# A 1536-row down projection moved from the start of a fused attention and GLU kernel into its dense end

## The chip, the cores and the metric

The kernel runs on one core of one Trainium2 chip. The metric is device time in microseconds (us) from launch to end; a run's time is compared with runs of the kernel before on the same chip. TensorE (PE) multiplies, with its weight loads (PEld) beside it; VectorE (DVE), ScalarE (ACT) and GpSimd (POOL) work elementwise; SyncE (SP) and GpSimd issue transfers (DMA), each from a queue of its own, in order.

## What is computed

```python
def _A_ref(x, k_cache, v_cache, wq, wo):
    B, Sq, D = x.shape                      # 1, 2048, 640
    Hq, Dh = 32, 192
    Hkv, Sk = k_cache.shape[1], k_cache.shape[2]
    W = min(4096, max(256, Sk // 4))        # 512
    ...
    scores = jnp.einsum("bhqd,bhkd->bhqk", q, k) * (Dh ** -0.5)
    p = _softmax(scores, axis=-1)
    o = jnp.einsum("bhqk,bhkd->bhqd", p, v)
    return (lambda x, *d: x.transpose(*d))(o, 0, 2, 1, 3).reshape(B, Sq, Hq * Dh) @ wo

def _B_ref(x, w_gate, w_up, w_down):        # D 640, F 1536
    g = jnp.einsum("bsd,df->bsf", x, w_gate)
    u = jnp.einsum("bsd,df->bsf", x, w_up)
    h = _sigmoid(g) * u
    return jnp.einsum("bsf,fd->bsd", h, w_down)

x = A_x
xn = _layernorm(x, axis=-1)
s = _A_ref(xn, A_k_cache, A_v_cache, A_wq, A_wo)
g = _silu(_B_ref(xn, B_w_gate, B_w_up, B_w_down))
return x + s * g
```

## The kernel before

The order of the work is written out by hand; every engine runs its instructions in program order.

The opening makes the gate g. It goes through four blocks of 512 rows (`s` = 0 to 3, loop over `NST`). In a block, twelve chunks of 128 hidden columns (`f`) are worked one after the other: ten matmuls into a pair of PSUM banks (line 469), a sigmoid on ScalarE (474), and on VectorE a product with the up half (475) into `hT_sb`, two buffers of which exist. Four bank pairs are used in turn, so TensorE's chunk f+4 waits for the VectorE product of chunk f. Then four row tiles of 128 rows go through the down projection (517): 24 matmuls each with `hT_sb` as the stationary operand, of 512 and 128 columns; sigmoid and product make the gate (524, 525), and GpSimd's queue writes it to `gB_d` in DRAM (541).

Other work is laid into these loops. The layer norm of the next block's four row tiles: statistics (`ln_stats`) at f = 5 to 8, the square root on ScalarE (`ln_rstd`, 352, with a table load before and after it) at f = 9, and at f = 10 and 11 the apply (359) and the transposes by DMA (428) into `xnT[s]`. Blocks 1 and 3 share one buffer `x_odd`; the apply has three output buffers, so the fourth apply waits for the first transpose. The largest absolute value of W_q is found in sixteen pieces of 1920 columns a partition (`scan_load`, `scan_fold`), all by VectorE; `set_scale` sends the per-partition result through DRAM to all partitions, and `set_scale2` makes of it a power of two, `w_up`, by which W_q goes to fp16. In block 3, W_q's first group is scaled and split: for each of its chunks ScalarE scales (240) and copies, VectorE makes sums (`sum_w`), and one more ScalarE copy (245) waits for such a sum. `swap` and `sum_x` prepare sums of x for a seven-product form of the query projection.

Attention runs in sixteen stages `r` (eight groups of heads g by two halves of the rows pi): query products (571), scores (665), exponent (669), values (679). Its output goes through transposes on SyncE's queue into `oT_d` in DRAM (`store_o`). ScalarE also sums the absolute values of W_o and v (724, 728), from which the scales of the dense end come.

The dense end multiplies the attention output by W_o. It takes sixteen steps m: eight pairs of row tiles for each half of the 6144 inner columns. A pair is a 2 by 2 block product made with seven products instead of eight (Winograd's form of Strassen's method), in fp16: four quads A11 to A22 (each 128 by 12 by 128) are loaded two steps ahead (`load_quads`), scaled by ScalarE (782), and summed by VectorE (`sum_quad`: S1 to S4); seven `product`s of twelve 320-column matmuls (950) fill three banks; `keep` (957) takes partial results out by ScalarE, `result` (969, 977, 979) adds them by VectorE. W_o's blocks are loaded, scaled and summed likewise (`load_op`, `scale_op`, `sum_op`). The first eight steps leave sums in `acc`; `prep` multiplies them by the gate read back from `gB_d` and adds x; the last eight finish the rows.

## Time and profile before

| | us |
|---|---|
| three runs: median (lowest to highest) | 878.44 (878.37 to 878.54) |
| the profiled execution, its own time | 878.02 |
| its span, first to last instruction | 876.2 |
| TensorE's mean granted clock | 1.000 |
| opening, up to the last down projection's end | 0 to 164.4 |
| attention | 164.4 to 689.4 |
| dense end | 689.4 to 876 |

In a list of groups a line reads: source line, engine, operation, output<-input, shapes, count, then busy time in us and mean ns of one. In a timeline it reads: start us, duration us, engine, line, operation, and in brackets the idle time of the engine just before and what ended it. Instructions of one engine overlap by about a tenth of a us, so the start of the next one tells what an instruction costs. A q after an engine's name is its transfer queue. The opening, by windows of ten us:

```profile
core 0: us, PE busy (x) PEld busy (x) DVE busy (x) ACT busy (x) POOL busy (x), PEclk, DMA share, GB/s
20.00:30.00 10.00, 10.00 (x48) 4.54 (x47) 7.03 (x17) 3.16 (x6) 0.00 (x0) 1.00 1.09 346
...
60.00:70.00 10.00, 10.00 (x48) 4.55 (x47) 9.75 (x15) 3.74 (x6) 0.09 (x1) 1.00 0.80 254
...
140.00:150.00 10.00, 10.00 (x48) 4.56 (x47) 8.21 (x14) 7.36 (x11) 1.19 (x2) 1.00 0.53 116
```

Columns are each engine's busy us and instructions, TensorE's granted clock, the mean busy share of the transfer engines and what they moved.

### The profile page before, as it was taken

Reading aid. Unit: us, or ns where it says so; the run is one execution under the profiler, and the core shown is the slowest. Engines: PE = TensorE matmul, PEld = TensorE weight load, DVE = VectorE, ACT = ScalarE, POOL = GpSimd, SP = SyncE. Lnnn points to the kernel's source line nnn. Section 1 sums busy time; section 2 is a strip of 40 time slices with the busy share of each in tenths; the row PEclk is TensorE's granted clock in tenths of the full one; section 3 lists DMA queues with packets and bytes.
Section 4 is the critical chain, followed back from the end, with each engine's and each line's share of the span. In section 5 each row is a group of like instructions: output and inputs, shape, how many; then the busy total and the mean of one; then the engine's idle time right before and its main releaser. Section 6 shows DMA issues by size and latency. Waiting matters only on the chain.

```text
span 876.2 us, 18804 instructions
## 1 busy us (share of the span) xinstructions
PE 870.4 (99%) x7605; PEld 564.1 (64%) x7605; DVE 670.4 (77%) x1088; ACT 576.7 (66%) x693; POOL 231.0 (26%) x326
## 2 busy tenths in 40 slices
PE   9999999999999999999999999999999999999998
PEld 5545454567757757757757757757757777777775
DVE  4879947677767767767767767777978868888986
ACT  4323347775887887797797797777485566666662
POOL 0050212582334334334334334334000000000000
PEclk9999999999999999999999999999999999999999
DMA  9994465229698898798898798689998998557641
GB/s 279 269 271 114 107 118 124 93 56 169 152 217 139 196 221 149 182 226 158 185 214 170 172 215 148 150 196 206 219 271 126 231 367 263 181 173 266 198 136 36
DMA packets 246935, 161.34 MB, mean 184 GB/s; under 512 B 158848, under 2 KB 231808, under 8 KB 246848
## 3 DMA queue, kind: packets, MB, share of 16 engines
q1 hardware_dynamic: 238304, 132.90, 62.3%
q0 software_dynamic: 8544, 27.24, 14.2%
q8 instruction: 59, 0.97, 0.5%
q14 instruction: 28, 0.23, 0.1%
HBM read 93.65 MB, written 30.41 MB: 142 GB/s over the span
## 4 chain that ended last, share of the span: by engine, by line
PE 98%; DVE 1%; DMA 0%; ACT 0%; issue 0%; DVEq 0%
PE ps_all L571 21%; PE ps_all L950 20%; PE ps_all L679 20%; PE ps_all L665 19%; PE ps_all L469 11%; PE ps_all L517 6%; PE ps_all L382 1%; DVE stats L344 0%; DVE arm L933 0%; DMA x_sb<-in_A_x_dram 0%; DVE arm L979 0%; DVE arm L977 0%; DVE xn L359 0%; ACT mid L397 0%; PE ps_all L395 0%
## 5 line engine op out<-in xcount | busy, mean ns | idle before, releaser
L669 ACT ACTIVATE E<-ps_all 128x1024 bf16<-128x1024 f32 x256 | 251.1, 1021 | 120.7 <-PE ps_all L665 120.0
L665 PE MATMUL ps_all<-qT,kT 64*128 64x512 bf16 x1536 | 198.2, 377 | 0.0
L679 PEld LDWEIGHTS <-E 128*128 128x128 bf16 x2048 | 169.7, 98 | 8.1 <-issue 8.1
L679 PE MATMUL ps_all<-v_sb,E 128*128 128x193 bf16 x2048 | 174.0, 247 | 0.0
L609 DVE TENSOR_TENSOR qT<-ps_all,qp 128x512 bf16<-128x512 f32 x174 | 115.5, 687 | 47.8 <-PE ps_all L571 36.5
L592 DVE COPY qp<-ps_all 128x512 f32<-128x512 f32 x150 | 100.6, 687 | 47.7 <-PE ps_all L571 47.6
L665 PEld LDWEIGHTS <-kT 64*128 64x128 bf16 x1536 | 84.9, 94 | 79.4 <-issue 4.4
L686 DVE TENSOR_TENSOR o_st<-ps_all,rden 128x768 bf16<-128x768 f32 x128 | 122.5, 957 | 4.4
L950 PEld LDWEIGHTS <-mid 128*128 128x128 f16 x996 | 97.3, 98 | 37.9
L571 PE MATMUL ps_all<-mid 64*128 64x512 f16 (+1 forms) x840 | 106.0, 376 | 0.0
L571 PE MATMUL ps_all<-mid,arm 64*128 64x512 f16 (+1 forms) x840 | 105.6, 376 | 0.0
L571 PEld LDWEIGHTS <-mid 64*128 64x128 f16 x840 | 48.8, 94 | 43.5 <-issue 1.2
L571 PEld LDWEIGHTS <-arm 64*128 64x128 f16 x840 | 47.0, 94 | 44.7 <-issue 0.3
L782 ACT ACTIVATE mid<-mid,w_sc 128x1536 f16<-128x1536 bf16 x41 | 63.4, 1571 | 0.0
L240 ACT ACTIVATE mid<-mid,w_sc 128x1536 f16<-128x1536 bf16 x37 | 58.2, 1572 | 0.6
L983 POOL DMA_DIRECT2D out_dram<-arm x14 | 7.6, 540 | 186.0 <-DVE arm L979 186.0
L474 ACT ACTIVATE sig_sb<-ps_all 128x512 bf16<-128x512 f32 x48 | 28.0, 596 | 40.2 <-PE ps_all L469 37.1
L226 POOL DMA_DIRECT2D mid<-in_A_wq_dram x80 | 48.1, 607 | 23.9 <-DVE mid L262 22.5
L517 PE MATMUL ps_all<-wd_sb,hT_sb 128*128 128x512 bf16 (+1 forms) x384 | 52.8, 299 | 0.0
L950 PE MATMUL ps_all<-arm,mid 128*128 128x320 f16 x348 | 51.0, 299 | 0.0
L475 DVE TENSOR_TENSOR hT_sb<-ps_all,sig_sb 128x512 bf16<-128x512 f32 x48 | 32.5, 682 | 22.7 <-PE ps_all L469 11.7
L950 PE MATMUL ps_all<-op,mid 128*128 128x320 f16 x336 | 48.3, 299 | 0.0
(162 smaller groups left out, 1047.6 us busy)
## 6 DMA issues: line engine op xcount, KB each, us to landing
oT_d<-oT SPq DMA_DIRECT2D x64, 384.0 KB, 5.0
mid<-oT_d SPq DMA_DIRECT2D x45, 384.0 KB, 4.6
mid<-in_A_wq_dram POOLq DMA_DIRECT2D x80, 192.0 KB, 6.5
arm<-in_A_wo_dram SPq DMA_DIRECT2D x16, 480.0 KB, 5.6
v_sb<-in_A_v_cache_dram SPq DMA_DIRECT2D x28, 192.0 KB, 6.0
kraw<-in_A_k_cache_dram SPq DMA_DIRECT2D x26, 192.0 KB, 4.2
mid<-in_A_wq_dram POOLq DMA_DIRECT2D x9, 480.0 KB, 7.8
kT<-oT_d SPq DMA_DIRECT2D x11, 384.0 KB, 5.1
```

The costliest lines, as they stand in the source:

```text
L240: nc.scalar.activation(raw.bitcast(F16), raw, AF.Copy, scale=w_up)
L469: nc.tensor.matmul(gu[:, i, :], lhsT=w[:, c, f * P:(f + 1) * P], rhs=xnT[s][:, c, :], start=(c == 0), stop=(c == NCD - 1),)
L517: nc.tensor.matmul(oB_ps[:, d0:d0 + dsz], lhsT=hT_sb[:, f, q * P:(q + 1) * P], rhs=wd_sb[:, f, d0:d0 + dsz], start=(f == 0), stop=(f == NF ...
L571: nc.tensor.matmul(ps_all[:, b, :], lhsT=w(r, c), rhs=x[r, c, :], start=(first and k == 0), stop=(k == len(cs) - 1), skip_group_check=True,)
L592: nc.vector.tensor_copy(dst, part(b))
L609: nc.vector.tensor_tensor(q_out(i, u, pp), part(b), t, ALU.add)
L665: nc.tensor.matmul(ps[:, b, :], lhsT=kT[h, c * PC + j, :], rhs=qT_t[r][i, j][h, pp, :], start=(j == 0), stop=(j == PC - 1),)
L669: nc.scalar.activation(E_t[r, i, pp][:, c, :, :], ps, AF.Exp, scale=scale_qk)
L679: nc.tensor.matmul(o_ps[:, q // 2, q % 2, 0:DH + 1], lhsT=E[:, c, h, q * P:(q + 1) * P], rhs=vt[:, c, 0:DH + 1], start=(c == 0), stop=(c = ...
L686: nc.vector.tensor_tensor(o_st[:, :, h * DH:(h + 1) * DH].rearrange("p (b i) d -> p b i d", b=2), o_ps[:, :, :, 0:DH], rden[:].to_broadcas ...
L782: eng.activation(t, t.bitcast(BF16), AF.Copy, scale=v_up)
L950: nc.tensor.matmul(ps_all[:, b, d0:d1], lhsT=a[:, c, :], rhs=w[:, c, d0:d1], start=(start and c == 0), stop=(c == KB - 1), skip_group_chec ...
```

## The change

Blocks 0 to 2 lose their down projection. Their `hT_sb` (now laid out by row tile) goes through SyncE's queue to twelve DRAM tensors `h_d`. The dense end gets six half-size steps "D" between the steps "O" that were there: a D step takes a pair of row tiles (0 and 4, 1 and 5, 2 and 6, 3 and 7, 8 and 9, 10 and 11) through the same seven products with half the inner length (`NH` = 6 matmuls of 320 columns a product), w_down scaled to fp16 and summed into seven blocks in the first two O steps. ScalarE applies Silu, GpSimd writes the gate. Block 3 keeps its down projection in bf16.

The scales for h and w_down come from sums of absolute values of w_up and w_down, eight scans on ScalarE in blocks 2 and 3, sent around by `set_scale` in attention stages 2 and 4. Of W_q's sixteen pieces twelve are now scanned by ScalarE (sums of absolute values) and four by VectorE. The layer norm of the next block, the x sums, w_down's load and the first k and v loads have new places.

```diff
-        sums = (4, 5, 6, 7, 9, 11), (2, 4, 7)
-        folds = {(0, 9): 0, (0, 10): 1, (0, 11): 2, (2, 0): 11, (2, 1): 12, (2, 2): 13, (2, 4): 14, (2, 5): 15}
-        folds_q = {(0, q): 3 + q for q in range(TQ)} | {(1, q): 7 + q for q in range(TQ)}
+        sums = {(1, 6): (0, 4), (2, 0): (0, 0), (2, 1): (0, 1), (2, 9): (0, 2), (2, 10): (0, 3), (2, 11): (0, 5),
+                (3, 2): (1, 0), (3, 4): (1, 1), (3, 7): (1, 2)}
+        folds = {(1, 0): 5, (1, 1): 6, (1, 9): 13, (1, 10): 14}
+        abs_in = [(0, 6), (0, 7), (0, 9), (0, 10), (0, 11), (1, 1), (1, 2), (1, 4), (1, 5), (1, 7), (1, 8), (1, 10)]
+        scan_act = dict(zip(abs_in, [i for i in range(NPC) if i not in folds.values()]))
+        abs_at = [(2, 1), (2, 2), (2, 4), (2, 5), (2, 9), (2, 10), (3, 4), (3, 10)]
+        ln_at = {0: (5, (1, 1, 2), 8), 1: (2, (1, 1, 1, 1), 6), 2: (2, (1, 1, 1, 1), 6)}
...
+        def scan_abs(i, col):
+            nc.scalar.activation(scan_t[i], scan_t[i], AF.Abs, accum_out=scans[:, col:col + 1])
+
+        def abs_hw(n):
+            v = wu_sb[:, :, 3 * n * P:3 * (n + 1) * P] if n < 4 else wd_sb[:, 3 * (n - 4):3 * (n - 3), :]
+            nc.scalar.activation(
+                scan_out.rearrange("p (c n) -> p c n", c=v.shape[1]), v, AF.Abs, accum_out=hw_sum[:, n:n + 1])
...
                 if s + 1 < NST:
                     t = (s + 1) * TQ
-                    if 5 <= f < 5 + TQ:
-                        ln_stats(t + f - 5)
-                    elif f == 5 + TQ:
+                    f0, counts, f1 = ln_at[s]
+                    n = f - f0
+                    if 0 <= n < len(counts):
+                        for q in range(sum(counts[:n]), sum(counts[:n + 1])):
+                            ln_stats(t + q)
+                    if f == f1:
                         ln_rstd(t, t + TQ)
-                    elif 5 + TQ < f <= 5 + TQ + TQ // 2:
-                        ln_rest(t + 2 * (f - 6 - TQ))
-                        ln_rest(t + 2 * (f - 6 - TQ) + 1)
+                    n = f - f1 - (1 if s else 0)
+                    if 0 <= n < 2:
+                        ln_rest(t + 2 * n)
+                        ln_rest(t + 2 * n + 1)
+                if (s, f) in sums:
+                    sum_x(*sums[s, f], sw)
...
+                if (s, f) in abs_at:
+                    abs_hw(abs_at.index((s, f)))
...
+                elif s == 2 and f == 0:
+                    set_scale(scans[:], mx_row)
+                elif s == 2 and f == 1:
+                    nc.sync.dma_start(wd_sb[:], B_w_down.rearrange("(f p) d -> p f d", p=P))
...
+            if s < NM3:
+                for q in range(TQ):
+                    nc.sync.dma_start(h_d[s * TQ + q][:], hT_sb[:, q, :, :])
+                continue
...
+    steps = [(k[0], int(k[1:])) for k in "O0 O1 D0 D1 O2 D2 D3 O3 D4 D5 O4 O5 O6 O7".split()]
+    steps += [("O", m) for m in range(8, 16)]
...
+        if r in (2, 4) and k == 7:
+            set_scale(*((hw_sum[:, 0:4], mx_rows[0], mx_h, 3) if r == 2 else (hw_sum[:, 4:8], mx_rows[0], mx_w, 4)))
...
+    def load_down(n, k, d):
+        nc.sync.dma_start(down_ops[n].bitcast(BF16), wd_r[:, k * NH:(k + 1) * NH, d])
+
+    def scale_down(n):
+        nc.vector.tensor_scalar(down_ops[n], down_ops[n].bitcast(BF16), wd_up, None, op0=ALU.mult)
+
+    def sum_down(n):
+        B11, T1, T2, B21, T3, B22, T4 = down_ops
+        a, b, c = ((T1, T3, B11), (T2, B22, T1), (T3, B22, T3), (T4, B21, T2))[n]
+        nc.vector.tensor_tensor(a, b, c, ALU.subtract)
...
+        if kind == "D":
+            if t not in gate_of:
+                gate_of[t] = turn_of(1, gate_rows)
+            if more is not None:
+                v = turn_of(2, down_tmps)
+                tt(v, ps, more[:], ALU.add)
+                ps = v
+            nc.scalar.activation(gate_of[t][:, d], ps, AF.Silu, scale=g_scale)
+            if (i, d) in ((0, RIGHT), (1, LEFT)):
+                nc.gpsimd.dma_start(gB_d[t * P:(t + 1) * P, :], gate_of[t])
+            return
...
+    for n, p in zip((0, 4, 5, 3), (1, 3, 6, 7)):
+        at("O0", p, scale_down, n)
+    for n, p in enumerate((1, 3, 3, 4)):
+        at("O1", p, sum_down, n)
+    for key, j in (("O2", 0), ("O2", 3), ("O3", 1), ("O4", 2)):
+        at(key, 0, load_op, 1, j)
+    for key, p, n in (("O3", 6, 0), ("O3", 8, 3), ("O4", 1, 4), ("O5", 1, 5)):
+        at(key, p, scale_op, 1, n)
+    for n, (key, p) in enumerate((("O4", 7), ("O5", 3), ("O6", 3), ("O7", 3))):
+        at(key, p, sum_op, 1, n)
+    prep_at = [("O2", 8), ("O3", 1), ("O3", 3)]
+    prep_at += [(f"O{m}", 8) for m in (4, 4, 5, 5, 6, 6, 7, 8, 9, 10, 11, 12, 13)]
...
+            if not small_:
+                names, eng = {0: ("A21",), 2: ("A11",), 4: ("A22", "A12")}.get(p, ()), nc.scalar
+            elif late:
+                names = {1: ("A21", "A22"), 3: ("A11",), 5: ("A12",)}.get(p, ())
+                eng = nc.vector if p == 1 else nc.scalar
+            else:
+                names, eng = ("A21", "A11", "A22", "A12") if p == 1 else (), nc.vector
+            for name in names:
+                scale_quad(j + 1, name, eng)
...
+        if j == 0:
+            for part_ in (0, 0, LEFT), (4, 0, RIGHT), (5, 1, RIGHT), (3, 1, LEFT):
+                load_down(*part_)
+        if j + 2 < NP:
+            load_quads(j + 2)
```

In the last piece, `at(step, place, ...)` lays a side task at a place of a step (the places lie behind the seven products), `scales` brings the next step's quads to fp16, and a D step before an O step is "late": it makes the next step's first product only after its own last.

## The prediction

> **What bounds the kernel now.** First the page: busy shares and the chain that ended last.
>
> ```profile
> PE 870.4 (99%) x7605; PEld 564.1 (64%) x7605; DVE 670.4 (77%) x1088; ACT 576.7 (66%) x693; POOL 231.0 (26%) x326
> PE 98%; DVE 1%; DMA 0%; ACT 0%; issue 0%; DVEq 0%
> ```
>
> TensorE never rests, so removed matmul time counts in full, and so does every pause that the change makes. Then the same chain in order of time (start, us, what). I call the four 512-row stages of the opening blocks 0 to 3; L469 is gate and up, L517 the down projection, L950 the dense end.
>
> ```profile
> 15.14 19.43 PE ps_all L469 x90
> 34.56 13.04 PE ps_all L517 x96
> 47.60 25.90 PE ps_all L469 x120
> ...
> 689.45 177.68 PE ps_all L950 x1308
> ```
>
> Each of the three L517 stages that go was 13.04 us in which ScalarE, VectorE and the queues got the next block ready. How they stand without it is read from the timelines of the opening: ScalarE around the end of block 0 and in block 3, SyncE's queue with the transposes (start, duration, queue, line; bracket: idle before and releaser).
>
> ```profile
> 29.21 0.60 ACT L474 ACTIVATE sig_sb<-ps_all 128x512 bf16<-128x512 f32 x1 [1.56 <-PE ps_all L469]
> 29.82 1.28 ACT L352 ACT_TABLE_LOAD   x1
> 31.12 0.30 ACT L352 ACTIVATE rstd<-mv,eps_t 128x4 f32<-128x4 f32 x1
> 31.43 1.28 ACT L474 ACT_TABLE_LOAD   x1
> ...
> 127.09 1.57 ACT L240 ACTIVATE mid<-mid,w_sc 128x1536 f16<-128x1536 bf16 x1
> ...
> 131.80 0.52 ACT L245 ACTIVATE mid<-mid 64x384 f16<-64x384 f16 x1 [1.42 <-DVE mid L259]
> ...
> 150.95 1.08 ACT L474 ACTIVATE sig_sb<-ps_all 128x512 bf16<-128x512 f32 x2
> ```
>
> ```profile
> 34.43 5.70 SPq L428 DMA_TRANSPOSE x_odd<-xn  x4
> 75.18 5.46 SPq L428 DMA_TRANSPOSE mid<-xn  x4
> ```
>
> Between 127.09 and 152.04 ScalarE's only idle times are four of 1.42 us, each for a VectorE result: in block 3 ScalarE with VectorE is a serial chain as long as TensorE's block. The price of one scan by ScalarE, from the attention stage:
>
> ```profile
> 244.27 1.80 ACT L724 ACTIVATE arm<-arm 128x1920 bf16<-128x1920 bf16 x1
> 245.98 0.19 ACT L724 ACTIVATION_READ_ACCUMULATOR arm<-arm 128x1 f32 x1
> 246.08 1.92 ACT L669 ACTIVATE E<-ps_all 128x1024 bf16<-128x1024 f32 x2
> ```
>
> The next instruction starts 1.81 us after the scan. Last, VectorE's timeline at the start of the dense end, where it now has 1.66 us to spare:
>
> ```profile
> 692.25 2.16 DVE L718 TENSOR_TENSOR mid<-mid,arm 128x3840 f16<-128x3840 f16 x1
> 696.07 0.49 DVE L969 TENSOR_TENSOR acc<-ps_all,p1s 128x320 f32<-128x320 f32 x1 [1.66 <-PE ps_all L950]
> ```
>
> **Matmuls.** Removed: 3 x 13.04 = 39.12 us. Added: 6 pairs x 7 products x 6 = 252 matmuls of 320 columns at 177.68/1308 = 0.1358 us: 34.23 us. Saving 4.89 us; the rest is what the moves cost.
>
> **A, end of block 0.** Block 1's matmuls wait for all four transposes into x_odd; they are now due at 34.56 and no longer at 47.60. The statistics end earlier (two tiles at f=7, 2 x 1.1 us on VectorE: 28.9), and the square root moves from behind f=9's sigmoid to f=8's. That sigmoid began at 27.05; the scans behind the sigmoids of f=6 and f=7 (22.73 + 2 x (0.5 + 1.8)) push it to 27.3. Then 0.6, table 1.3, root 0.3: 29.5; reciprocal and first apply: first transpose issued at 30.2. From that issue to the last landing before took 41.5 - 34.43 = 7.1 us in block 0 (the last was issued at 38.9, landing 2.6) and 82.0 - 75.18 = 6.8 in block 1, since the fourth apply waits for the first transpose's buffer. So 37.0 to 37.3: pause 2.6 us. Bounds 2.0 and 3.5 (the first transpose stands in SyncE's queue behind seven scan loads; without w_down ahead these end about 5.4 us earlier, the time from x_sb4's landing at 21.7 to w_down's at 27.1, but GpSimd's scan loads now share the engines).
>
> **B and C, ends of blocks 1 and 2.** With scans behind f=1, 2, 4 and 5 the sigmoid of f=6 starts at T+14.3 (T: start of the block); two table loads and the root 2.9, its own 0.6, f=7's sigmoid and multiply 1.3, apply 0.5: first transpose at T+19.65, last landed 6.8 later, T+26.45 against 25.9. Pause 0.55 each; bounds 0 and 1.2.
>
> **D, block 3.** Its chain on ScalarE starts with L240, which needs w_up. Before, w_up was set 5 us ahead of the block (five small operations, 1.05 us). Now VectorE reaches f=9's multiply of block 2 at about T+22.0 and has 3 x (0.6 + 1.48), multiplies and x sums, and 1.05 behind it: w_up at T+29.3, 3.4 us into block 3 where L240 stood at 1.6. Late by 1.8. Two scans of w_down stand in the chain (f=4, f=10): 3.6. The chain ended with f=11's multiply at 152.87, and its last use in the first L517 row tile comes after 22 of 24 matmuls, 151.38 + 2.99 = 154.37: 1.5 us of cover. Pause 1.8 + 3.6 - 1.5 = 3.9. Bounds: w_up in time, 2.1; w_up 3.1 late and a scan at its full 2.0, 5.6. Queued behind the late ScalarE: sigmoids, hence multiplies, hence TensorE's banks and its lhsT.
>
> **E, first step of the dense end.** VectorE's list gets two scalings of w_down quarters ahead of its first result. Their loads stand in SyncE's queue behind the last stores of oT, so are issued where the next loads were, 695.5; first landing 4.3 us on (oT_d loads there: median 4.4), each further 0.49 MB at 0.37 MB/us 1.3: 699.8 and 701.1. A scaling, between 0.61 (1536 columns) and 1.21 (3840), is 0.71: VectorE free at 701.8 = 12.3 after 689.45; two results 0.9, first sum 0.95: 14.2. TensorE wants that sum after 8 products of 12 matmuls, 13.04: pause 1.2, bounds 0.3 and 2.5.
>
> **At nothing.** Scans, folds and set_scale of W_q, the k and v loads moved to GpSimd's queue at the end of block 1, and w_down's load (12.5 us to land) at block 2: needed 10 us or more later. 12 stores of h (SyncE, 0.39 MB each) replace 12 gate stores on GpSimd and wait for each block's last multiply; behind them stand the swap copies, landing about T+9, as their first sum in block 3 comes up. The multiply into hT_sb writes four runs of 128 in place of 512; the row stays 0.68, and twice that would still end within a chunk's 2.16 us outside block 3. Two set_scale and set_scale2 pairs in attention: VectorE about 1.3 us each in a stage where it is 7/10 busy; GpSimd waits up to 9.8 us in a part where it waited 20 us and more for ScalarE; uncovered, 2 us. Half-size step of the dense end, 42 matmuls = 5.70 us: VectorE 4 scalings (0.416, the 768-column row) + 4 sums (0.56, between 0.36 at 384 and 0.95 at 1536) + 3 results 0.49 = 5.36; before a full step 1.23 + 3.81 + 1.47 = 6.51. Full steps four and five: 1.21 + 2.15 + two prep pairs 3.40 + 3.81 + 1.47 = 12.04 against 11.41. These overruns (0.8 three times, 0.63 twice) are covered by the 3 us between the next sums and their need and by slacker steps; uncovered 3.7 us. ScalarE has 6.2 at most in a half step and rests in others. Loads of 384 KB a quad take 4.6 us and are issued two steps ahead.
>
> **Sum.** -4.89 + 2.6 + 0.55 + 0.55 + 3.9 + 1.2 = +3.9. The profiled execution took 878.02 (span 876.2 and 1.8 around it): 881.9. The median of the runs is 0.4 above it: **882.3**. With all lower bounds the median comes to 877.9, with all upper ones to 887.5. No part can gain beyond the matmuls: TensorE has no idle time to give back.
>
> **Rivals.** Forecast, 0.46: own range 880.5 to 885.0.
> 1. Not slower, 0.20: block 3's chain ends before its last use, at its start plus 28.9. For it: the page gives ScalarE 7 tenths there, and the four waits are 5.7 us together. Against: they are waits for results of that chain. Decides: f=11's multiply. D = 0: **878.4**.
> 2. The saving comes whole, 0.14: the order that I read makes none of the pauses, since TensorE's records show no wait now. Against: the row of 6.8 us. **873.5**.
> 3. VectorE becomes the bound in the dense end, 0.11: the 3.7 us above add: **886.0**.
> 4. A pause slows what follows, 0.09. After the start, nine 512-column matmuls took 4.02 us where 120 of L469 take 25.90, 0.447 against 0.216: 2.1 us lost. Twice (A, D): **886.5**. Against: the granted clock reads 1.00 even there, and D comes in parts. The Trainium skill, TensorE: Matmul & The Clock Gate, section Part 1: The HAM clock gate, says that the clock halves after an idle window of about 3.4 us; by that rule A would be too short. No pause of the trace can show it.
>
> Faster by over 0.2% (1.8 us, about what runs of this kernel can tell from no change): 0.14 (rival 2). Within: 0.20 (rival 1). Slower: 0.66. The range reaches from 876.1, the lower bounds less the 1.8 us, to the upper bounds' 887.5; it leaves out rival 2 and little else.
>
> **What would show it.** PE idle in front of the first matmuls of block 1 (2.6 us, released by the transposes), of blocks 2 and 3 (0.5), inside block 3 and its first L517 tile (3.9, released by VectorE), and in front of the second step of the dense end (1.2). The half steps at 5.7 us each. Wrong if TensorE's idle time stays under 2 us, or if the half steps take 6.5.

## The result, and the profile after

The changed kernel took **910.07 us** (median of four runs, 899.6 to 911.63), the kernel before 878.4: ratio **1.0336 [1.0258, 1.0414]**, slower. The forecast was slower, at 882.3. So the sign held and the size did not: +31.7 us where +3.9 was expected. The four runs of the changed kernel lie 12 us apart, those of the kernel before 0.6, so the totals of its variants below say less than their waits, and each wait is read in one profiled execution. The profiled execution took 908.94 (span 906.8, against 876.2). From the page: the rows of the engines, the clock granted in the 40 slices, and the chain that ended last by engine.

```profile
PE 874.4 (96%) x7569; PEld 569.5 (63%) x7569; DVE 675.5 (74%) x1134; ACT 624.1 (69%) x770; POOL 235.1 (26%) x330
...
PEclk9899899999999999999999999999999999999999
...
PE 83%; DMA 7%; issue 3%; DVE 3%; ACT 2%; SPq 0%; POOL 0%; DVEq 0%; POOLq 0%; ACTq 0%
```

TensorE has 36 matmuls fewer, as the edit says, and yet is 4.0 us longer busy, although 4.89 us of matmuls went: some of them ran slowly. And transfers, which held next to nothing of the chain, now hold 7% of it. Where, the chain in order of time tells (start, us, what):

```profile
15.77 6.49 PE ps_all L486 x30
30.82 5.45 DMA x_odd<-xn
36.84 4.94 DMA x_odd<-xn
41.91 26.57 PE ps_all L486 x110
68.86 2.59 DMA mid<-xn
71.50 19.72 PE ps_all L486 x91
91.22 9.43 DMA x_odd<-xn
116.03 15.62 DMA kraw<-in_A_k_cache_dram
...
150.52 4.67 PE ps_all L606 x40
...
569.85 9.78 DMA kraw<-in_A_k_cache_dram
...
687.19 5.71 DMA arm<-in_B_w_down_dram
694.49 38.48 PE ps_all L1010 x282
...
759.19 5.87 DMA gB_d<-op
771.99 125.69 PE ps_all L1010 x924
```

(L486 is gate and up, L441 the transposes, L560 the down projection that stays, L606 the queries, L714 the values, L1010 the dense end.) What TensorE waited for, by line and releaser (us in total, times, longest):

```profile
PE ps_all L486 <- DMA x_odd<-xn: 13.2, 2, 6.7
PE ps_all L560 <- DVE hT_sb L492: 3.0, 3, 2.0
PE ps_all L1010 <- DVE acc L1059: 2.6, 1, 2.6
PE ps_all L714 <- DVE qT L644: 2.3, 1, 2.3
PE ps_all L1010 <- ACT p1s L1017: 2.0, 1, 2.0
PE ps_all L486 <- DVE hT_sb L492: 1.4, 1, 1.4
...
PE ps_all L486 <- DMA mid<-xn: 0.9, 1, 0.9
```

The stages end at 150.5 (opening), 680.5 (attention) and 906.8. Without any pause the opening would end at 164.43 - 39.12 = 125.3, so it lost **25.2 us**; attention took 529.95 against 525.0 and lost 4.9; the dense end took 226.3 against 186.75 + 34.23 = 221.0 and lost 5.3. Together 35.5, less the 4.89 saved: the 30.6 of the span. Of the opening's 25.2, the pauses in front of blocks 1, 2 and 3 (A, B and C of the prediction) make 6.72, 0.87 and 6.45, the waits in block 3 (D) 4.4, matmuls at half speed 5.0 (below) and a later start 0.6; some 1.2 is in smaller pieces.

The pauses are not all. TensorE's timeline behind the first of them, then the same in windows (columns: stretch, length, busy us of PE, PEld, DVE, ACT, POOL with their counts, granted clock, DMA share, GB/s):

```profile
41.91 2.29 PE L486 MATMUL ps_all<-x_odd,wg_sb 128*128 128x512 bf16 x5 [6.72 <-DMA x_odd<-xn]
44.00 2.34 PE L486 MATMUL ps_all<-x_odd,wu_sb 128*128 128x512 bf16 x5
46.13 1.83 PE L486 MATMUL ps_all<-x_odd,wg_sb 128*128 128x512 bf16 x5
47.80 1.24 PE L486 MATMUL ps_all<-x_odd,wu_sb 128*128 128x512 bf16 x5
```

```profile
36.00:40.00 4.00, 0.00 (x0) 0.00 (x0) 1.64 (x3) 2.33 (x4) 1.74 (x2) 1.00 1.08 290
40.00:44.00 4.00, 2.09 (x6) 0.74 (x6) 0.00 (x0) 0.00 (x0) 0.00 (x0) 0.56 1.07 297
44.00:48.00 4.00, 4.00 (x12) 1.51 (x11) 1.26 (x2) 0.60 (x1) 0.00 (x0) 0.58 1.02 403
48.00:52.00 4.00, 4.00 (x20) 1.84 (x19) 2.81 (x4) 4.00 (x5) 0.97 (x2) 1.00 1.06 268
```

Five matmuls take 2.3 us where they take 1.24, at a granted clock of 0.56 to 0.58. The first fifteen take 47.80 - 41.91 = 5.89 us where fifteen take 3.24: 2.65 us lost behind the pause. The same happens behind the long pause at the end of block 2 (clock 0.50 between 104 and 108), where fifteen take 5.56: 2.32 us lost. This time at half speed is most of the rise in TensorE's row.

The pause at the end of block 2 (91.22 on) shows in two queues. First GpSimd's timeline, then SyncE's, then VectorE's fourth apply:

```profile
78.43 0.55 POOL L213 DMA_DIRECT2D mx_d<-w_sc  x1 [18.33 <-DVE w_sc L212]
88.92 0.54 POOL L214 DMA_DIRECT2D mx_row<-mx_d  x1 [9.94 <-DMA mx_d<-w_sc]
89.44 3.73 POOL L230 DMA_DIRECT2D mid<-in_A_wq_dram  x6
```

```profile
91.22 11.20 SPq L441 DMA_TRANSPOSE x_odd<-xn  x4
```

```profile
100.74 0.45 DVE L372 TENSOR_SCALAR xn<-x_sb,mv,rstd 128x640 bf16<-128x640 bf16 x1 [8.28 <-DMA x_odd<-xn]
```

W_q's raw loads were to be issued from 76 to 82. They stand on GpSimd's queue behind the two steps of W_q's scale: its 128 maxima, 4 bytes a partition, are stored, and the store took 9.94 us to land. So six loads of 192 KB go out at 89.4 to 93.2, right around the transposes at 91.22. The first three of these land in 8.2 to 9.5 us; the fourth apply, whose buffer the first transpose frees, starts after 8.28 us of idle, and its transpose, alone by then, lands in 2.6.

At the same place the kernel before was not quiet either: GpSimd's timeline there, and the landings of the four transposes.

```profile
115.36 0.55 POOL L210 DMA_DIRECT2D mx_row<-mx_d  x1 [7.13 <-DMA mx_d<-w_sc]
```

```profile
L428 SPq DMA_TRANSPOSE x_odd<-xn x4: 1207/1252/1383, 113.9 to 117.9; - x4
...
DMA to landing us min/median/max: 2.6/4.9/5.8
```

Until a gate row's store at 121.63, the only transfer of the program beside them was the read-back of W_q's scale (64 KB, landed 4.1 us after its issue), and three of the four took 4.9 to 5.8.

### The profile page after: what moved, and what is told of

It is laid out like the page before. It is cut to its first block, busy times and chain, and to the rows that moved or that the text cites. A ratio compares the mean times of both kernels' runs of the same rounds, so it can differ in the third digit from the quotient of the medians.

```text
span 906.8 us, 18988 instructions
## 1 busy us (share of the span) xinstructions
PE 874.4 (96%) x7569; PEld 569.5 (63%) x7569; DVE 675.5 (74%) x1134; ACT 624.1 (69%) x770; POOL 235.1 (26%) x330
## 4 chain that ended last, share of the span: by engine, by line
PE 83%; DMA 7%; issue 3%; DVE 3%; ACT 2%; SPq 0%; POOL 0%; DVEq 0%; POOLq 0%; ACTq 0%
PE ps_all L606 20%; PE ps_all L714 19%; PE ps_all L1010 19%; PE ps_all L700 18%; PE ps_all L486 6%; DMA kraw<-in_A_k_cache_dram 3%; DMA x_odd<-xn 2%; PE ps_all L560 1%; DMA gB_d<-op 1%; DVE hT_sb L492 1%; PE ps_all L395 1%; DMA arm<-in_B_w_down_dram 1%; DMA x_sb<-in_A_x_dram 0%; ACT mid L301 0%; ACT sig_sb L491 0%
## 5 line engine op out<-in xcount | busy, mean ns | idle before, releaser
L714 PE MATMUL ps_all<-v_sb,E 128*128 128x193 bf16 x2048 | 175.8, 248 | 2.3 <-DVE qT L644 2.3
L714 PEld LDWEIGHTS <-E 128*128 128x128 bf16 x2048 | 171.1, 98 | 10.8 <-issue 10.6
L1010 PEld LDWEIGHTS <-mid 128*128 128x128 f16 x1176 | 115.0, 98 | 49.9 <-issue 5.4
L700 PEld LDWEIGHTS <-kT 64*128 64x128 bf16 x1536 | 84.9, 94 | 79.4 <-issue 4.4
L606 PE MATMUL ps_all<-mid 64*128 64x512 f16 (+1 forms) x840 | 106.4, 376 | 0.4 <-DVE qT L644 0.4
L606 PE MATMUL ps_all<-mid,arm 64*128 64x512 f16 (+1 forms) x840 | 105.6, 376 | 0.0
L606 PEld LDWEIGHTS <-mid 64*128 64x128 f16 x840 | 49.0, 94 | 44.1 <-issue 2.1
L606 PEld LDWEIGHTS <-arm 64*128 64x128 f16 x840 | 47.2, 94 | 44.7 <-issue 0.5
L1010 PE MATMUL ps_all<-arm,mid 128*128 128x320 f16 x462 | 67.5, 299 | 2.0 <-ACT p1s L1017 2.0
L830 ACT ACTIVATE mid<-mid,w_sc 128x1536 f16<-128x1536 bf16 (+1 forms) x41 | 60.2, 1493 | 0.0
L244 ACT ACTIVATE mid<-mid,w_sc 128x1536 f16<-128x1536 bf16 x37 | 58.2, 1572 | 2.7 <-DVE w_sc L222 1.7
L1010 PE MATMUL ps_all<-op,mid 128*128 128x320 f16 x378 | 55.1, 299 | 0.0
L1010 PE MATMUL ps_all<-mid 128*128 128x320 f16 x336 | 48.4, 299 | 2.8 <-DVE acc L1059 2.6
L486 PEld LDWEIGHTS <-wg_sb 128*128 128x128 bf16 x225 | 22.4, 101 | 43.3 <-issue 17.9
```

What stands on the lines that cost most here:

```text
L244: nc.scalar.activation(raw.bitcast(F16), raw, AF.Copy, scale=w_up)
L486: nc.tensor.matmul(gu[:, i, :], lhsT=w[:, c, f * P:(f + 1) * P], rhs=xnT[s][:, c, :], start=(c == 0), stop=(c == NCD - 1),)
L606: nc.tensor.matmul(ps_all[:, b, :], lhsT=w(r, c), rhs=x[r, c, :], start=(first and k == 0), stop=(k == len(cs) - 1), skip_group_check=True,)
L700: nc.tensor.matmul(ps[:, b, :], lhsT=kT[h, c * PC + j, :], rhs=qT_t[r][i, j][h, pp, :], start=(j == 0), stop=(j == PC - 1),)
L714: nc.tensor.matmul(o_ps[:, q // 2, q % 2, 0:DH + 1], lhsT=E[:, c, h, q * P:(q + 1) * P], rhs=vt[:, c, 0:DH + 1], start=(c == 0), stop=(c = ...
L830: eng.activation(t, t.bitcast(BF16), AF.Copy, scale=up)
```

## The experiments

All ratios are to the kernel before, run beside each kernel on the same chip (medians 878.1 to 878.4).

**1. Four buffers for the applied rows.** Without the fourth apply's wait, what is left of A and C is the landing alone.

```diff
-        xpool = bctx.enter_context(tc.tile_pool(name="xpool", bufs=3))
+        xpool = bctx.enter_context(tc.tile_pool(name="xpool", bufs=4))
```

> Only the output buffers of the layer norm's apply become four instead of three, so the fourth apply and its transpose no longer wait for the landing of the first. Theory 1 (the pauses of 6.7 and 6.5 us in front of blocks 1 and 3 are two transfer times in series, because the fourth transpose stands behind the first): the fourth is issued right behind the third, at 34.6 instead of 36.8 and at 95.0 instead of 101.2 us; the two pauses shrink by 2 to 3 us each, the time by 4 to 6 us. Theory 2 (the transposes themselves are slow, 5.5 and 9.5 us to land instead of 2.6, because loads keep the transfer engines busy): the first transposes land as late as before and all four share the same engines; the two pauses shrink by less than 1.5 us each, the time by less than 3 us.

895.37 (893.4 to 896.93), ratio 1.0172 [1.0133, 1.0210]: 14.7 us came back, more than expected. A is 5.65 (from 6.72), so it shrank as the second theory had it; C is 3.46 (from 6.45), as the first had it, with half speed only for a part behind it; L560's waits fall to 1.62. Some 4.2 of the 14.7 is attention (525.7), which the edit does not touch. The transposes are still slow (block 0 4.6 to 5.6 us, block 2 4.2 to 8.0). So the wait for the buffer only multiplied slow landings.

**2. The loads moved away from the transposes.** W_q's pieces 5 and 6 behind block 0's transposes; the raw loads ahead of the scale on GpSimd's queue.

```diff
-        for i in range(NSB):
+        for i in range(NSB - 2):
...
+                if (s, f) == (0, NF - 1):
+                    for i in range(NSB - 2, NSB):
+                        scan_load(i, nc.sync)
...
+                    for c in range(3):
+                        load_raw(0, c, nc.gpsimd)
...
-                if s == 2 and 2 <= f < 5:
-                    load_raw(0, f - 2, nc.gpsimd)
```

> Only loads move. Block 0: two of the seven first W_q pieces and the reloads of four are issued behind the transposes instead of ahead of them. Block 2: the six raw W_q loads are issued on GpSimd's queue ahead of the scale's round trip through DRAM (whose store took 9.9 us to land behind w_down's load) instead of behind it, so at about 74 instead of 89.4 us. Theory 2 (loads on the same transfer engines make the transposes land late): the first transposes land in about 3 us instead of 5.5 and 9.5; the pause in front of block 1 falls from 6.7 to about 2.6 and that in front of block 3 from 6.5 to about 0.5 us, the half-speed matmuls behind them (2.3 us each) go too, and the time falls by 12 to 15 us. Theory 1 (only the waiting fourth transpose counts): the time falls by less than 4 us. Against both: the later reloads may make ScalarE wait in block 1.

912.54 (911.88 to 913.35), 1.0371 [1.0329, 1.0413]: no gain, but a clear picture. A fell to 4.83 (first landing 3.25) and C to 1.34 (landings 2.6 to 4.0), and B grew from 0.87 to 16.30 (TensorE's timeline):

```profile
84.60 2.31 PE L487 MATMUL ps_all<-mid,wg_sb 128*128 128x512 bf16 x5 [16.30 <-DMA mid<-xn]
```

The raw loads, now ahead of the scale, had nothing to wait for and went out at 63 to 68, into block 1's transposes, which landed in 10.0 to 19.0 us. The slow landings follow the loads from one block's end to another's.

**3. Filler matmuls.** 24 products of zeros ahead of blocks 1 and 3, to keep the clock up through the pauses.

```diff
+                    if f == 0 and s in (1, 3):
+                        for _ in range(24):
+                            nc.tensor.matmul(gu[:, 0, :], lhsT=warm[:, 0:P], rhs=warm[:], start=True, stop=True)
```

> 24 matmuls of 512 columns on a tile of zeros (24 x 0.216 = 5.2 us) are put in front of the first matmul of blocks 1 and 3, where TensorE stood still for 6.7 and 6.5 us; nothing waits for them. Theory (a pause halves the granted clock, and the next 10 to 12 matmuls run at half speed): the clock reads 1.00 behind both pauses, the first ten matmuls of each block take 2.2 instead of 4.3 us, the time falls by 4 to 5 us. Rival (these matmuls are slow for another reason, the transfers that are under way): they stay at 0.43 us each and the time stays within 1.5 us.

916.27 (912.73 to 920.28), 1.0412 [1.0364, 1.0460]. It tells nothing of the clock: in this run the transposes landed later (up to 10.4 and 12.7 us), 6.6 and 3.5 us stayed idle behind the filler, and the matmuls after them ran at half speed again. Why they landed later was not found. It did show a loss in attention. GpSimd's timeline, then SyncE's, then TensorE's:

```profile
317.75 0.57 POOL L213 DMA_DIRECT2D mx_d<-w_sc  x1 [5.88 <-DVE w_sc L212]
329.97 0.56 POOL L214 DMA_DIRECT2D mx_all<-mx_d  x1 [11.65 <-DMA mx_d<-w_sc]
```

```profile
319.02 1.13 SPq L158 DMA_DIRECT2D kraw<-in_A_k_cache_dram  x2
```

```profile
334.14 6.09 PE L717 MATMUL ps_all<-v_sb,E 128*128 128x193 bf16 x50 [7.50 <-DVE qT L647]
```

The k load issued 1.3 us after the store of w_down's scale (4 bytes a partition, one of the two pairs costed at nothing) landed at 331, a microsecond after that store and 12 us from its issue; VectorE's k scaling waited for it in front of the queries' sums. Attention took 538.3.

**4. The second k load early.** It goes straight behind the first k scaling of block 3.

```diff
+                        if f == 0:
+                            load_k((0, 1), nc.gpsimd)
...
-                    if f == 2:
-                        load_k((0, 1), nc.gpsimd)
```

> Block 3: the second k load is issued right behind the scaling that frees its buffer, ahead of the raw W_q loads on GpSimd's queue, at about 110 instead of 115.5 us. Theory D1 (VectorE's two waits for this load, 2.1 and 1.0 us, are what makes the last hidden chunks late): these waits go, the pauses between 130 and 141 us (1.4 + 0.5 + 0.5 + 2.0) fall by 3 us together, the time by about 3 us. Theory D2 (the chain of ScalarE and VectorE with the late w_up and the two w_down scans is as long anyway, as the prediction had it): the waits go, but the pauses fall by less than 1 us.

902.27 (899.74 to 906.76), 1.0257 [1.0210, 1.0304]. VectorE's wait for k is gone; L560's waits are 1.17 and 1.96 = 3.1 where block 3's were 4.4, a gain of 1.3 between the two theories. That does not divide D into its parts: in run 1, where the scans, w_up and the k load stand as in the changed kernel, block 3's waits were 1.62. A 6.82, B 2.33, C 3.76: the other ends vary from arrangement to arrangement.

**5. Four parts together.** Runs 1 and 4, the scale pairs in stages 3 and 5 of attention, and w_down's quarters for the dense end loaded in the last stage of attention.

```diff
-        if r in (2, 4) and k == 7:
+        if r in (3, 5) and k == 1:
...
+            if k == 4:
+                for n, kk, d in (0, 0, LEFT), (4, 0, RIGHT), (5, 1, RIGHT), (3, 1, LEFT):
...
-        if j == 0:
-            for part_ in (0, 0, LEFT), (4, 0, RIGHT), (5, 1, RIGHT), (3, 1, LEFT):
-                load_down(*part_)
```

> Four parts, each read in its own stage: four apply buffers and the early k load (both as tried alone); in attention the two new scales go around in stages 3 and 5 instead of 2 and 4, where no k load is issued; the four w_down loads of the dense end are issued in attention's last stage instead of behind the last stores. Theories: (a) the store of a scale (128 partitions x 4 bytes, 9 to 12 us to land) holds up the k load issued beside it (7 to 11.7 us instead of 2.4 to 6), and TensorE's waits in attention come from there: attention takes 525.0 to 526.0 us and no k load of groups 2 and 3 takes over 7 us; rival: they come from elsewhere and such landings are found again. (b) the pause in the first dense step (2.0 to 2.6 us) is the late w_down loads alone: it goes, and the dense end takes 222 to 223 us instead of 224 to 226.5; rival: the banks or ScalarE make it wait anyway. (c) the opening takes 139 to 140.5 us (141.8 with four buffers alone, less 1.5 to 3 for the k load), against 125.3 that its matmuls need. Together 887 to 890 us.

903.36 (897.89 to 907.37), 1.0277 [1.0228, 1.0326]. The wait at the first dense step (E) is gone: dense end 221.5. But the parts did not add up: A 7.51, C 6.27, and attention 534.1 although the k loads of those two stages landed within 4.8. Its waits are others (2.7 for VectorE, 1.8 for ScalarE). Up to 276.5 VectorE and ScalarE stood still for 3.9 and 3.1 us, for something that the trace does not place on this core. One thing stands beside it: a transfer of instructions (16 KB) that began at 266.6, while a scale's store was under way, took 8.8 us, where such transfers took about 1 in run 1. Run 7 shows the same pair (8.5 us, and both engines still up to 274.2). That the engines waited for it is not shown.

**6. Nine loads less.** The later nine pieces of W_q are not loaded: the scan reads the first pieces twice, so W_q's maximum is not that of the whole matrix.

```diff
-                            scan_load(i + NSB, nc.gpsimd)
+                        scan_t[i + NSB] = scan_t[i]
```

> Left out: the nine later W_q loads of the scan (4.4 MB on GpSimd's queue between 26 and 54 us); the scans run over the first seven pieces again, so the time is that of the same work with these transfers away. Theory (loads that share the transfer engines make the transposes late): the pause in front of block 1 falls from 6.7 to 3 to 4.5 us (two pieces from SyncE's queue still run into it), in front of block 2 from 0.9 to under 0.5; the one in front of block 3 stays at 6 us or so, because the six raw loads issued 2 us ahead of its transposes are still there. Rival (the transposes' own queue or the apply sets it): pauses as before, within 1 us.

907.9 (902.93 and 912.87), 1.0333 [1.0267, 1.0400]. **A fell from 6.72 to 2.44**, near the 2.6 that was forecast (this run's block 0 began 5.3 us later, and all its times with it); its four transposes landed in 2.6 to 2.7:

```profile
42.74 1.99 PE L486 MATMUL ps_all<-x_odd,wg_sb 128*128 128x512 bf16 x5 [2.44 <-DMA x_odd<-xn]
```

B is 0.19; C, where the six raw loads still go out at 89.4, is 10.42. So A's excess is those loads. Even behind this shorter pause five matmuls took 1.99 us in place of 1.24. Attention lost 9.7 us in this run, 6.6 of it again behind a k load beside a scale's store (landing 11.5 to 14.1).

**7. The loads re-laid, store kept.** From run 5 (so with four buffers and the early k load): pieces held until behind block 0's transposes, the raw loads directly behind the scale's store, scans moved to match.

```diff
+                    nc.gpsimd.dma_start(mx_d[0][:].rearrange("o p -> p o"), mx)
+                    for c in range(3):
+                        load_raw(0, c, nc.gpsimd)
+                    load_k((0, 0), nc.gpsimd)
```

> The four parts, and the opening's loads laid out so that none should be under way with the transposes: x of block 1 ahead of the last weights, layer norm of block 1 one chunk earlier, five W_q pieces instead of seven ahead of the first transposes and all reloads behind them, scans of block 1 later, raw W_q and first k loads between the scale's store and its read-back, v loads in block 3, all w_down scans in block 2, the scale's arithmetic one chunk earlier. Theory (contention, not capacity): pauses of 0 to 1 us in front of block 1, up to 1.5 in front of blocks 2 and 3, up to 1.6 in block 3; the opening takes 128 to 131 us, the time is 877 to 881 us. Rival (capacity: the same bytes in 39 us less; moving loads moves the waits, as the run with quiet loads showed): one pause of over 4 us appears elsewhere in the opening, which takes 136 us or more, the time 885 us or more.

896.88 (890.15 to 898.75), 1.0194 [1.0152, 1.0236]; opening 142.9, attention 532.5, dense end 221.5. A 4.23, B 0.96, C 5.55: the raw loads, issued behind the store (72.6), took 13.7 to 16.1 us, w_down's load 25, and ScalarE's scan of it waited 9.9; that scan, ahead of a sigmoid, is this C. Again the store, again what is issued next to it.

**8. No stores.** From run 7: the scale's maximum reaches all partitions by one matmul (ones by a diagonal of the maxima, into PSUM) in place of store and broadcast.

```diff
+        def to_diag(v, m):
+            nc.vector.tensor_reduce(m, v, axis=mybir.AxisListType.X, op=ALU.max)
+            nc.vector.tensor_scalar(diag[:], ident[:], m, None, op0=ALU.mult)
+        def spread():
+            ps = bank2()[:, 0, 0:P]
+            nc.tensor.matmul(ps, lhsT=ones_t[:], rhs=diag[:], start=True, stop=True)
```

> A version meant to keep the saving. The three cross-partition scales are spread by one small TensorE matmul each (ones times a diagonal) instead of a store and a broadcast read through DRAM; w_up is scanned in blocks 0 and 1; W_q's reloads in block 0 are queued behind one that has to wait until the transposes are issued, two pieces are loaded behind the transposes of block 1; w_down, raw W_q and the first k load go through SyncE's queue in block 2; four apply buffers, early k load and early w_down loads as before. Theory (what is left are transfers that slow each other, the 4-byte stores of the scales first): pauses in front of blocks 1, 2, 3 of at most 1, 2 and 1 us, opening 128 to 132 us, attention 524.9 to 526 us without a wait for k, dense end 221.5 us; 877 to 881 us in all. Rival (the opening has too many bytes for its 125 us, wherever they are put): one of these pauses is over 4 us again, the opening takes 136 us or more, 885 us or more.

890.34 (888.51 to 894.2), 1.0154 [1.0127, 1.0180]. Attention 525.5, near the 525.0 of before; block 0's transposes land in 2.6 to 3.6 and A is 1.44. B is 4.34 with half speed behind it, and the spread's bank waits 2.77 for VectorE in block 3.

**9. Store or queue?** Two kernels from the changed one: (a) the raw loads on SyncE's queue, issued at 76.8 to 80.9 with the store at its side; (b) the same with W_q's scale spread by a matmul, no store.

```diff
-                    load_raw(0, f - 2, nc.gpsimd)
+                    load_raw(0, f - 2, nc.sync)
```

> One part: the six raw W_q loads of block 2 go through SyncE's queue, so they are issued at about 77 to 81 us and no longer wait on GpSimd's queue for the scale's store. The store (128 partitions x 4 bytes) stays and is issued at about the same time. Theory S (while such a store is under way, other transfers crawl): the raw loads take over 11 us to land, w_down's load over 16 us, and the pause in front of block 3 stays over 3 us. Theory R (only the late issue of the raw loads, 2 us ahead of the transposes, made these late): the raw loads land within 9 us and the pause falls from 6.5 to under 1.5 us.

> As the run before, and W_q's scale is spread over the partitions by one TensorE matmul instead of the store and the broadcast read, so no 4-byte store is under way in block 2. Theory S: raw loads within 9 us, w_down's load within 14 us, the pause in front of block 3 under 1.5 us, where the run before keeps over 3. Theory R: both runs alike in these. In both, w_up is ready before block 3, so the waits in block 3's last chunks shrink by 1 to 2 us against the changed kernel.

902.17 (895.68 and 908.67; 1.0274 [1.0188, 1.0359]) and 899.68 (897.5 and 901.87; 1.0245 [1.0217, 1.0274]). C's pause is 1.66 and 1.11 where it was 6.45. The raw loads, seen by their line in (a), then in (b) (issue ns min/median/max, first and last start; landing):

```profile
L230 SPq DMA_DIRECT2D mid<-in_A_wq_dram x6: 607/662/1375, 76.8 to 80.9; - x6
...
DMA to landing us min/median/max: 12.3/12.8/13.8
```

```profile
L230 SPq DMA_DIRECT2D mid<-in_A_wq_dram x6: 605/642/1371, 76.3 to 80.4; - x6
...
DMA to landing us min/median/max: 8.8/9.2/9.4
```

Same loads, same queue, same time: beside the 512-byte store a load takes 3.6 us longer (w_down's 13.8 against 9.5; it took 13.0 in the changed kernel, beside the store and without raw loads). From 84 to 88 us, with loads in flight in both, the transfer engines moved 142 and 112 GB/s in (a) and 232 and 234 in (b). But C's cost in the changed kernel is mainly *when* the loads go out: with the store kept, (a) has 1.66, where the theory of the store expected over 3.

**10 and 11. Toward a version that keeps the gain.** From run 8, W_q's last four pieces behind block 1's transposes and one raw load behind block 2's; then scans and folds re-placed and two more gate rows.

```diff
-                    later.extend(i + NSB for i in sorted(done) if i + NSB < NPC - 2)
+                    later.extend(i + NSB for i in sorted(done) if i + NSB < NPC - 4)
...
+    gate_rows += [acc[order[13]][:].bitcast(BF16)[:, n * D:(n + 1) * D] for n in range(2)]
```

> The version before it (e8) with its four remaining pauses taken one by one: W_q's last four pieces are loaded behind the transposes of block 1 and scanned in block 2 (so block 1 has 3.4 MB of pieces to load instead of 4.4), the first two W_q scans come before the layer norm's square root instead of around it, the first k load and the third raw load go behind the transposes of block 2, and w_down's scale is spread in the down projections of block 3. Theory (what was left were transfers and waits in the wrong place, not capacity): pauses in front of blocks 1, 2, 3 of at most 1, 1.5 and 1 us (they were 1.4, 4.3 with half-speed matmuls behind it, and 1.7), none of 2.8 in block 3; opening 127 to 130 us, attention 525 to 526, dense end 221.5 to 222.5; 876 to 880 us. Rival (capacity): the loads moved into block 2 make w_down or the transposes there late, one pause of over 3 us appears, 883 us or more.

> The version before it (e10), in which all twelve transposes landed within 3.4 us, with three more places changed: in block 0 no W_q scan stands ahead of the sigmoid of chunk 8 (one there instead of two before the layer norm's square root, three w_up scans ahead), the four VectorE scans of W_q come at the end of block 1, so the layer norm does not wait 3.5 us for a piece, and the gate has five row buffers instead of three. Theory: pauses in front of block 1 under 0.8 us (2.2 before), in front of block 2 under 1 us with no half-speed matmuls behind it (3.1 before), no wait of the dense end's second matmul group for the gate's stores (0.9 before); opening 128 to 129.5 us, attention 525 to 526, dense end 221 to 222; 877 to 879.5 us, so within 0.2% of the kernel before. Rival: ScalarE, now full for the first half of block 1, or VectorE at its end, makes a new wait of over 1.5 us there; 881 us or more.

885.31 (882.59 to 886.24; 1.0066 [1.0040, 1.0092]) and 879.21 (878.35 to 883.66; 1.0014 [1.0003, 1.0025]). In run 10 all twelve transposes land within 3.4 us; left are pauses behind a late layer norm (A 2.16, B 3.13 with the clock at 0.69 and 0.74 behind it). In run 11 no pause is over 1.5, and the dense end runs its 1560 matmuls without a break in 221.0: the second wait of the changed kernel there, for a gate row's store, is gone with five rows in place of three (0.9 in run 10; runs 5 and 7 had none with three, so it also depends on the moment).

**12 and 13. The last two microseconds.** The layer norm of blocks 1 and 2 one chunk earlier; then the first spread two chunks later, out of VectorE's way.

```diff
-        ln_at = {0: (4, (1, 1, 2), 7), 1: (2, (1, 1, 1, 1), 6), 2: (2, (1, 1, 1, 1), 6)}
+        ln_at = {0: (4, (1, 1, 2), 7), 1: (1, (1, 1, 1, 1), 5), 2: (1, (1, 1, 1, 1), 5)}
...
-                if (s, f) in ((2, 2), (2, 7)):
+                if (s, f) in ((2, 4), (2, 7)):
```

> The version before it (e11) with one edit: in blocks 1 and 2 the layer norm of the next block starts one chunk earlier (statistics at chunks 1 to 4, square root at 5, transposes from 6 or 7 on). Theory (what is left in front of blocks 2 and 3, 0.9 and 1.5 us, is the length of the layer norm and of four quiet transposes, the prediction's terms B and C, and can be moved forward): these pauses go to 0 to 0.3 and 0 to 1 us, the opening falls from 130.5 to 128 to 129.5, the time to 876.5 to 878.2 us, so the saving begins to show. Rival (the transposes of block 2 then start while w_down's load, which landed 0.4 us after they were issued, is still under way): the pause in front of block 3 stays over 1.5 us and the time within 0.5 us of 879.2.

> The version before it (e12) with the small matmul that spreads w_up's scale two chunks later in block 2; there TensorE waited 2.0 us for VectorE, which was behind with W_q's last scans and the statistics, now one chunk earlier. Theory (this wait is all that took the place of the pauses removed in e12): it goes, no other of over 1 us appears in the opening, which takes 128 to 129.3 us; the time is 876.3 to 877.5 us, 0.1 to 0.2% under the kernel before. Rival (VectorE is the bound of block 2 by now, and its lateness comes out in another wait): the opening stays at 130 us or more and the time at 878.3 to 879.2.

878.69 (878.2 to 880.49; 1.0003 [0.9995, 1.0012]) and 878.19 (877.87 to 878.95; **0.9998 [0.9989, 1.0007]**): the same as before. Run 12 lost C and got 1.99 in front of the spread; run 13 lost that and got C back at 1.42: its transposes went out behind VectorE from 81.86 on, as in run 11 (81.89), though the layer norm stands a chunk earlier. Run 13's page and its waits:

```profile
PE 866.1 (99%) x7572; PEld 566.9 (65%) x7572; DVE 675.9 (77%) x1138; ACT 623.8 (71%) x770; POOL 222.7 (25%) x312
```

```profile
PE ps_all L500 <- DMA x_odd<-xn: 1.4, 1, 1.4
...
PE ps_all L500 <- issue: 0.6, 1, 0.6
PE ps_all L500 <- DMA mid<-xn: 0.5, 1, 0.5
```

TensorE's busy time is 4.3 us under before's 870.4, which is the 4.89 less the spreads and what else moved; the opening's end, 129.7, is still 4.4 above 125.3. There the gain goes. The likely reading, not tested by itself, is that without the three L517 stages VectorE's and ScalarE's work of the opening has 39 us less to hide under: moving one piece out of the way put another in it, twice.

## Why the prediction was right or wrong

**Matmuls (-4.89): right.** The 1560 matmuls of the dense end took 221.0 in runs 11 to 13, which is 186.75 + 34.23; run 13's busy TensorE agrees.

**A (2.6, upper bound 3.5): wrong, 6.72.** The issue was foreseen (30.2; 30.82 came, after a root that ended at 30.1 for a forecast 29.5). What failed is "From that issue to the last landing before took 41.5 - 34.43 = 7.1 us": it now took 36.84 + 4.94 - 30.82 = 11.0. The row came from a stretch in which the last of W_q's pieces were landing (until 37.5) and none was issued behind them; now five more go out on GpSimd's queue between 26.1 and 38.6. The transposes land in 4.6 to 5.6 us in place of 2.6 to 3.7, and twice in a row, because of the buffer. SyncE's seven pieces, which were to "end about 5.4 us earlier", ended at 35.9, 1.6 earlier. The sentence "GpSimd's scan loads now share the engines" stood only beside an upper bound that gave it under 1 us. With the loads out (run 6) A is 2.44.

**B (0.55): near, 0.87**, but by luck of what was in flight: 16.30 and 4.34 in runs 2 and 8.

**C (0.55): wrong, 6.45.** The mechanism was on the list "at nothing", where W_q's set_scale and w_down's load were "needed 10 us or more later"; the raw loads behind set_scale on GpSimd's queue were not named. Need was weighed; what else these transfers slow while in flight was not, nor that a load's place on GpSimd's queue is behind a store that takes ten microseconds. The trace of before had it: its store of the same maxima took 7.4 us. The row was short, too. The 6.8 us from first issue to last landing, used for B and C, came from the end of block 1, where the last transpose, issued at 79.4, landed in 3.3 and not in the 2.6 that was added: 7.5. At C's own place the row was 117.9 + 4.9 - 113.95 = 8.9, and with it C would have been forecast at some 2.6.

**D (3.9): its size near (4.4), its parts not shown.** The k load, which had been put at nothing, made about 1.3 (run 4); how much of the rest is the scans and w_up is open, since run 1 has 1.62 with all of them in place. So rival 1, no pause in block 3, did not come either.

**E (1.2, upper bound 2.5): 2.61.** Landings and VectorE's list came as forecast (VectorE free 13.1 us after the start for 12.3). "TensorE wants that sum after 8 products" was wrong: it stopped 11.4 us after the start (691.88), for a bank that the two results (0.48 each) behind the scalings free, and not for the sum.

**The rest of what stood at nothing.** Attention lost 4.9: half of it (2.34) behind the k load of 569.85, which went out 1.0 us ahead of W_o's own scale store and took 9.78 to land; the remainder is the clock behind that pause and small waits. The kernel before has that store too, but there the k load went out 2.5 us ahead of it and landed in 4.6. Over the other runs k loads issued 1 to 2 us ahead of such a store took from 4.2 to 14.1, so what decides is open. That the new pairs can do the same is shown by runs 3 and 6, and without their stores attention took 525.4 or 525.5 in every run (8 and 10 to 13); with them it took 525.7 (runs 1 and 2) to 538.3. The gate row's store cost 2.04 in the dense end: ScalarE's Silu waits for one of three rows. VectorE's overrun of 3.7 (rival 3) did not come: the dense end of runs 11 to 13 is unbroken.

**Rival 4, that a pause slows what follows, was right** and had 0.09; 2.65 and 2.32 us were lost behind two pauses, for 2.1 each forecast. Over all sixteen traces, from 20 us on, half speed stood behind every pause of 3.13 us and more and behind 11 of the 28 pauses from 1.6 to 3.1 us, and behind no shorter one that stood alone. The shortest with half speed behind it was 1.76 (attention, run 5), the longest without 3.07 (attention, run 3). In the changed kernel half speed lasted 6.8, 6.8 and 3.4 us (from 40.5, 101.9 and 583.2). The Trainium skill, TensorE: Matmul & The Clock Gate, section Part 1: The HAM clock gate, gives an idle window of about 3.4 us and says that it runs freely. The lengths agree with such a window, once or twice; the pauses do not, since some from 1.76 to 3.13 us were enough, so there the measurement decides. A pause of 2.6 us, as forecast for A, was not safe by its size: the 2.44 of run 6 had half speed behind it.

**Rival 2 (873.5)** was reached by no version; the best is at 878.2.

Not settled: the unexplained stretches of runs 5 and 7 in attention, the parts of D, why run 3's transposes landed so late, and by what a 512-byte store slows its neighbours.

## What to carry to other kernels

When work that hid other work is moved away, price not only whether each transfer lands in time but what it slows while in flight: write down, for every latency-bound transfer on the path (here twelve transposes), which loads are issued within 10 us of it. A queue's order is no schedule: an issue goes out when what it waits for is done, so a load behind a slow round trip comes late, and one with nothing to wait for comes early. And a small saving of matmuls is worth having only if the pauses it opens stay short: here half speed came behind every pause over 3.1 us and behind 11 of 28 between 1.6 and 3.1, and cost another 2.3 and 2.65 us behind the two longest of the changed kernel.

## What the runs showed of the hardware

- Transposes of 128x640 land in 2.6 us in quiet, in 4.6 to 5.6 beside pieces of 480 KB (block 0 of the changed kernel) and in 8.2 to 9.5 with six raw loads of 192 KB issued in the same few us (its block 2), up to 14.5 and 19.0 in runs 6 and 2. Beside little but the read-back of a scale three took 4.9 to 5.8 (the kernel before).
- Raw loads beside the scale's store were slow from either queue: 12.3 to 13.8 us from SyncE's (run 9a), 13.7 to 16.1 from GpSimd's (run 7). This agrees with the Trainium skill, DMA: Bandwidth & Descriptors, section Issuing engines are not separate DMA queues, by which all issuers' transfers interleave on the same 16 DMA engines.
- A store of 128 x 4 bytes takes 7.4 to 10.1 us to land in the kernel before and 6.6 to 12.1 in the other runs, and a load beside it 12.8 in place of 9.2 (run 9). The Trainium skill, DMA: Bandwidth & Descriptors, section Latency and other measured facts, puts the fixed cost of a transfer at some 2 us; these stores are far from it.
- One matmul of ones by a diagonal spreads a column of maxima over the partitions without a transfer, at the cost of a bank and two VectorE operations.
